# One deferred step for the four state sums of a pair, and a new place for the last two pairs of a retention + bilinear feed-forward kernel

## The chip, the cores and the metric

The kernel runs on one core of one Trainium2 chip. The metric is the device time of one execution in microseconds (us). Four runs of the kernel before gave 336.97, 335.21, 335.25 and 334.94 us: a median of 335.23 us, from 334.94 to 336.97.

TensorE is called PE below, and its weight loads PEld; VectorE is DVE, ScalarE is ACT, GpSimd is POOL, and SyncE, which issues most of the DMAs here, is SP.

## The reference

Two operations in a row. First a retention layer (attention without softmax, with a decay per head) over 8 batches, 8 heads, 576 positions and a head size of 64:

```
scores = (q @ k^T) / 8
ret    = (scores * gamma_h ** (i - j) for i >= j, else 0) @ v       # per batch and head
```

Its output is laid out as 4608 tokens (8 batches x 576) of 512 features and goes into a feed-forward layer without activation:

```
out = ((x @ w_a) * (x @ w_b)) @ w_out        # 512 -> 1536 -> 512
```

All inputs and the output are float32 in DRAM.

## The kernel before

**Tiles.** The tokens are worked on in 18 *pairs* of 256 tokens. A batch has 576 = 2 x 256 + 64 positions, so pairs 0 to 15 are the two halves of each batch (pair n is half n % 2 of batch n // 2), and pairs 16 and 17, from `LEFT` on, gather the last 64 positions of batches 0 to 3 and 4 to 7. `rows_of` (L48) tells for each pair which rows of which batch it holds: two runs of 128 rows for a regular pair, four runs of 64 rows for a left one. A load (`load_pair`, L124) or a store (`store`, L627) issues one DMA per run, tensor and column part.

**Retention by states.** The 256 tokens of a pair are four blocks of 64. Inside a block the kernel uses masked scores; what comes from earlier blocks of the batch enters through a running sum of k^T v, the *state*. For a pair n, `keyed` (L475) makes the four k^T v products of the pair in two PSUM tiles, `kv0` and `kv1` (32 small matmuls, L489). Four instructions of DVE, `add(0)` to `add(3)`, then make the running sums in `sums`: `add(i)` reads the product of block i (`kv0` for i = 0 and 2, `kv1` for i = 1 and 3) and sum i - 1 (L506 for the first block of a batch, L509 for the others). ACT casts the sums to bf16 `states`: sum 1, and sum 3 for the next pair or for the left pairs, in `convert` (L516, L518, L520), and sums 0 and 2, with the partition halves exchanged, in `convert_swapped` (L513). `matched` makes the scores (`sc`, L545), which DVE masks (`sT`, L554); `from_states` (L571) and `from_keys` (L584) make the retention output `o` of a pair, which DVE scales into `xT` (L594). A left pair has nothing to sum: `keyed` returns at once for it, and its states come from `left_states`.

**Feed-forward.** `ffn_block` works on blocks of 512, 256, 256 and then seven times 512 tokens. For each of the 12 slices F of the hidden size: four matmuls into a PSUM tile `pa` (L664), cast by ACT into `ha` (L672); four matmuls into `pb` (L679), multiplied by DVE with `ha` into `hT` (L684). Then, for each 128 tokens, 12 matmuls into `po` (L699), copied by ACT or DVE into `osb` (L708, L710) and stored (L635, L637). The very last 128 tokens are done in two halves of 256 columns, each stored by itself.

**PSUM.** `pa`, `pb`, `po`, `kv0`, `kv1` and the transposes of the start take their space from one pool, `ps_ffn`, of four buffers. A tile takes the buffer whose last reader stands earliest in the recorded order; its first matmul waits for the last reader of the tile that had that buffer. While `kv0` and `kv1` wait for their adds, the feed-forward has the other two buffers.

**Order.** The order of all instructions is written out by hand. PE's queue is that of the feed-forward; `todo` holds the retention work with due times counted in matmuls of 512 columns, and at the edges of the feed-forward what is due is put in. `stretch(into, outof)` (L602) is one such piece: the states part of pair `outof`, then the products and scores of pair `into`, then the keys part of `outof`. From pair 8 on there are two stretches per block: one 116 matmuls before the start of the next block, among its `pa`/`pb` slices, which takes in an odd pair, and one 44 before, among `po`, which takes in an even one. What a stretch leaves for DVE and ACT goes into the list `later` as *deferred steps*, in this order: adds 0 and 1; adds 2 and 3; scaling of `o` (two steps); `convert` with the first mask; `convert_swapped` with the second mask. `pop()` takes one step from the list. In blocks of 512 tokens it is called twice per slice F: after the matmuls of `pa`, before the cast to `ha` is recorded, and after the multiplication into `hT`. In the first three blocks it is called only after `hT`. In `po` it is called after matmuls 3, 6 and 9 and after the copy. The engines run their instructions in the order in which they were recorded; so a step that is popped earlier stands earlier in the queues of DVE and ACT.

Of the kernel before, what the change touches and what calls it, by code (L numbers as in the profile page):

```python
# [18 lines left out]
def kernel(  # L19
# [10 lines left out]
    nc = tc.nc  # L30
# [9 lines left out]
    gammas = [1.0 - 2.0 ** (-5.0 - h) for h in range(H)]  # L40


    NP = NTOK // 256
    LEFT = 2 * B
    FIRST = 3
    assert S == 9 * 64 and B == 8

    def rows_of(n):  # L48

        if n < LEFT:  # L50
            return [(kp, 0, 128, n // 2, 256 * (n % 2) + 128 * kp)
                    for kp in (0, 1)]
        return [(i // 2, 64 * (i % 2), 64, 4 * (n - LEFT) + i, S - 64)
                for i in range(4)]

    def pool(name, bufs, space=None):
# [193 lines left out]

    natural, transposed, scored = {}, {}, {}
    sums_of = {}
    states_of = {LEFT + i: left_states[:, i] for i in (0, 1)}
    later = []

    def pop():
# [77 lines left out]
    def state_step(i, behinds):  # L334

        n, hh = STEPS[i]
        kv = ps_ffn.tile([128, 2, 2, 64], FP32, tag="ab", name="kv0")
        fresh = {0, 1}
        for behind in behinds:
            parts = [(n - 1, slice(0, 128))] if n % 2 else []  # L340
            parts.append((n, slice(0, 128) if behind else half(0)))
            for m, rows in parts:
                qkb, vb = natural[m, hh]
                for j in (0, 1):
                    for kp in (0, 1):
# [12 lines left out]
        if which:  # L358
            w = into[n, which[0]]
            for r in (0, 1):  # L360
                nc.scalar.copy(
                    state_after[half(r), w:w + len(which), cs, half(r)],
                    kv[half(r), which[0]:which[-1] + 1])
        if (n, behinds[-1]) == (1, 1):
            nc.scalar.copy(left_states[:, 0, 0, cs], kv[:, 1])
        elif (n, behinds[-1]) == (FIRST - 1, 1):
            if FIRST not in states_of:
                sums_of[n] = sum_pool.tile([128, 4, HP, 64], FP32,
                                           tag="sums", name="sums")
                states_of[FIRST] = state_pool.tile(  # L370
                    [128, 4, HP, 64], BF16, tag="states", name="states")
            nc.vector.tensor_copy(sums_of[n][:, 3, cs], kv[:, 1])
            nc.scalar.copy(states_of[FIRST][:, 0, cs], kv[:, 1])

    def output_step(i, place=None):
# [41 lines left out]

    def block_of(n, i):

        return 4 * (n % 2) + i if n < LEFT else 8  # L420

    def ahead(n):


        qf, kf, vf = paired.pop(n)
        qkb = nat.tile([128, 2, 2 * DM], BF16, tag="qkb", name="qkb2")
        vb = nat.tile([128, 2 * DM], BF16, tag="vb", name="vb2")
        for w, t in ((0, qf), (1, kf)):
            nc.gpsimd.tensor_copy(qkb[0:64, w], t[0:64])  # L429
            to = qkb[64:128, w].rearrange("p (j r d) -> p j r d", r=2, d=D)  # L430
            fro = t[64:128].rearrange("p (j r d) -> p j r d", r=2, d=D)
            for r in (0, 1):
                nc.gpsimd.tensor_copy(to[:, :, 1 - r], fro[:, :, r])  # L433
        nc.gpsimd.tensor_tensor(  # L434
            vb.rearrange("p (k h d) -> p k h d", k=2, h=H),
            vf.rearrange("p (k h d) -> p k h d", k=2, h=H),
            vs2[:, n % 2 if n < LEFT else 2].unsqueeze(3).to_broadcast([128, 2, H, D]),
            op=ALU.mult)
        natural[FIRST + n, "pair"] = (qkb, vb)

# [25 lines left out]
    def of(store, n):  # L466
        return store[FIRST + n, "pair"]
# [7 lines left out]
    def keyed(n):  # L475


        if n >= LEFT:
            return (lambda: None,) * 2
        qkb, vb = of(natural, n)  # L480
        kvs = [ps_ffn.tile([128, 2, HP, 64], FP32, tag="ab", name=f"kv{a}")
               for a in (0, 1)]
        begun = Begun()
        for kp in (0, 1):
            for c in range(HP):
                for a, r in QUADS:
# [8 lines left out]
        sums_of[n] = sums  # L495
        if n % 2 == 0:
            states_of[n] = state_pool.tile([128, 4, HP, 64], BF16,
                                           tag="states", name="states")
            states_of[n + 1] = state_pool.tile([128, 4, HP, 64], BF16,
                                               tag="states", name="states")  # L500
        into, batch = states_of[n], n // 2

        def add(i):
            own = kvs[i % 2][:, i // 2]
            if block_of(n, i) == 0:
                nc.vector.tensor_copy(sums[:, i], own)  # L506
            else:
                prev = sums[:, i - 1] if i else sums_of[n - 1][:, 3]
                nc.vector.tensor_tensor(sums[:, i], own, prev, op=ALU.add)  # L509

        def swapped(to, fro):
            for r in (0, 1):
                nc.scalar.copy(to(half(1 - r)), fro(half(r)))  # L513

        def convert():
            nc.scalar.copy(into[:, 2], sums[:, 1])  # L516
            if n % 2 == 0:
                nc.scalar.copy(states_of[n + 1][:, 0], sums[:, 3])  # L518
            elif batch % 2 == 0:
                nc.scalar.copy(left_states[:, batch // 4, batch % 4],  # L520
                               sums[:, 3])

        def odd_ones(t, r, i):
            return t[r].rearrange("p (k a) c d -> p a k (c d)", a=2)[:, i]

        def convert_swapped():
            swapped(lambda r: odd_ones(into, r, 1),
                    lambda r: odd_ones(sums, r, 0))
            if n % 2 and batch % 2:
# [47 lines left out]
    def from_keys(n, o, begun):  # L577
        vb = of(natural, n)[1]
        sT = of(scored, n)
        for c in range(HP):  # L580
            for kp in (0, 1):
                for a, r in QUADS:
                    v0 = kp * DM + c * 128 + 64 * r
                    nc.tensor.matmul(o[half(r), a, c, kp, :],  # L584
                                     vb[half(a), v0:v0 + 64],
                                     sT[half(a), r ^ a, c, kp, :],
                                     start=begun.first(a, r), stop=True,
                                     skip_group_check=True)
        s0 = 64 * block_of(n, 0)
        step = 128 if n < LEFT else 0  # L590
# [297 lines left out]
```

## Time and profile before

| | before |
|---|---|
| median of four runs | 335.23 us |
| the profiled execution, its own time | 336.97 us |
| its span in the trace | 335.3 us |
| PE busy | 327.2 us (98%) |
| DVE busy | 162.8 us (49%) |
| ACT busy | 128.0 us (38%) |
| POOL busy | 114.9 us (34%) |
| adds of states, L506 and L509 | 6 x 424 ns and 46 x 424 ns (medians) |
| multiplication into hT, L684 | 120, mean 633 ns |
| cast to ha, L672 | 120, mean 542 ns |

The profiled execution is the one of 336.97 us, the slowest of the four; 1.7 us of it lie around the span. A matmul of the trace has the time from its start to the end of its result, and the next one starts before that end; so PE counts as busy where it in fact waits a little. How fast PE goes is read from the starts: four 512-column matmuls of a `pa` or `pb` take 0.86 us from the first start to the start of what follows, four of 256 columns 0.43 us.

### The profile page before, as it was taken

The page shows a single profiled execution, that of the slowest core. Times are in us where ns is not written, and L with a number is a line of the kernel's source. Part 1 is how long each engine was busy: PE and PEld are TensorE (multiplying, and loading weights), DVE is VectorE, ACT ScalarE, POOL GpSimd, SP SyncE. Part 2 cuts the span into 40 slices and gives each one's busy share as a digit, 9 for nine tenths or more (in the row PEclk, how much of TensorE's full clock was granted, in tenths as well). Part 3 has the DMA queues.
Part 4 walks back from the last instruction along what each step waited for, and adds up shares of the span by engine and source line. Part 5 has one row for each costly group of instructions (what it writes and reads, how often), then busy time and mean ns, then how long its engine had stood idle before and what let it go on. Part 6 is the DMA issues. An engine that isn't in the chain of part 4 may idle for free.

```text
span 335.3 us, 8707 instructions
## 1 busy us (share of the span) xinstructions
PE 327.2 (98%) x3648; PEld 168.5 (50%) x3648; DVE 162.8 (49%) x292; ACT 128.0 (38%) x275; POOL 114.9 (34%) x146
## 2 busy tenths in 40 slices
PE   7999999999999999999999999999999999999994
PEld 4644446857644554545454545454544444444443
DVE  5724445466746465566246624762475145314420
ACT  7634743444525244353235323532262123213311
POOL 4770068550547468445054505450420000000000
PEclk9979999999999999999999999999999999999999
DMA  7999999997999999993599259955850510020014
GB/s 210 252 162 207 253 232 220 217 170 118 202 198 226 225 215 254 229 214 81 132 228 208 54 136 234 168 78 148 178 115 2 143 47 0 2 104 23 1 31 94
DMA packets 143191, 50.37 MB, mean 150 GB/s; under 512 B 124592, under 2 KB 138672, under 8 KB 143152
## 3 DMA queue, kind: packets, MB, share of 16 engines
q1 hardware_dynamic: 138400, 45.10, 65.9%
q0 software_dynamic: 4752, 4.72, 8.6%
q8 instruction: 28, 0.46, 0.6%
q14 instruction: 11, 0.09, 0.1%
HBM read 37.75 MB, written 9.44 MB: 141 GB/s over the span
## 4 chain that ended last, share of the span: by engine, by line
PE 92%; SPq 2%; DMA 2%; ACT 1%; DVE 0%; issue 0%; ACTq 0%; DVEq 0%
PE po L699 28%; PE pb L679 28%; PE pa L664 28%; SPq L142 2%; DMA vf<-in_v_dram 2%; PE o L584 2%; PE o L571 1%; PE sc L545 1%; PE kv L489 1%; PE pa L646 1%; PE kv L348 1%; PE o L398 1%; PE o L389 0%; ACT vb L296 0%; ACT osb L708 0%
## 5 line engine op out<-in xcount | busy, mean ns | idle before, releaser
L684 DVE TENSOR_TENSOR hT<-ha,pb 128x512 bf16<-128x512 bf16 (+1 forms) x120 | 75.8, 633 | 99.2 <-PE pb L679 90.1
L672 ACT CAST ha<-pa 128x512 bf16<-128x512 f32 (+1 forms) x120 | 64.7, 542 | 125.6 <-PE pa L664 124.9
L679 PE MATMUL pb<-xT,wb_sb 128*128 128x512 bf16 (+1 forms) x480 | 111.8, 358 | 0.1
L664 PE MATMUL pa<-xT,wa_sb 128*128 128x512 bf16 (+1 forms) x474 | 110.3, 358 | 0.2
L699 PE MATMUL po<-wo_sb,hT 128*128 128x512 bf16 (+1 forms) x444 | 97.5, 374 | 0.0
L679 PEld LDWEIGHTS <-wb_sb 128*128 128x128 bf16 x480 | 46.7, 98 | 47.6 <-issue 1.6
L664 PEld LDWEIGHTS <-wa_sb 128*128 128x128 bf16 x474 | 45.3, 98 | 46.0 <-issue 1.3
L699 PEld LDWEIGHTS <-hT 128*128 128x128 bf16 x444 | 42.2, 98 | 46.9
L429 POOL CAST qkb<-qf 64x1024 bf16<-64x1024 f32 x15 | 15.5, 1031 | 91.3 <-DMA qf<-in_q_dram 75.5
L710 DVE COPY osb<-po 128x512 f32<-128x512 f32 (+1 forms) x18 | 12.2, 676 | 42.0 <-PE po L699 42.0
L434 POOL TENSOR_TENSOR vb<-vf,vs 128x1024 bf16<-128x1024 f32 x15 | 28.5, 1902 | 9.6 <-PE o L584 5.3
L708 ACT COPY osb<-po 128x512 f32<-128x512 f32 (+1 forms) x19 | 10.9, 574 | 47.5 <-PE po L699 47.5
L594 DVE TENSOR_TENSOR xT<-o,qs 128x512 bf16<-128x512 f32 x30 | 19.6, 682 | 7.1 <-PE o L584 7.1
L509 DVE TENSOR_TENSOR sums<-kv,sums 128x256 f32<-128x256 f32 x46 | 19.4, 422 | 1.7
L554 DVE TENSOR_TENSOR sT<-sc,mask 128x512 bf16<-128x512 f32 x30 | 19.7, 680 | 0.0
L433 POOL CAST qkb<-kf 64x512 bf16<-64x512 f32 x30 | 17.7, 616 | 0.8
L433 POOL CAST qkb<-qf 64x512 bf16<-64x512 f32 x30 | 17.6, 616 | 0.6
L429 POOL CAST qkb<-kf 64x1024 bf16<-64x1024 f32 x15 | 15.5, 1036 | 3.6 <-DMA kf<-in_k_dram 3.0
L513 ACT CAST states<-sums 64x512 bf16<-64x512 f32 x26 | 16.0, 617 | 0.4
L288 POOL CAST qkb<-kf 128x512 bf16<-128x512 f32 x5 | 3.1, 616 | 18.9 <-DMA kf<-in_k_dram 18.9
L723 PE MATMUL w<-ones 128*128 128x256 bf16 (+1 forms) x36 | 7.8, 342 | 1.5 <-DVE ones L186 1.5
L328 DVE TENSOR_TENSOR sT<-sc,mask_s 128x1024 bf16<-128x1024 f32 x6 | 7.3, 1220 | 1.7 <-PE sc L320 1.7
(81 smaller groups left out, 158.3 us busy)
## 6 DMA issues: line engine op xcount, KB each, us to landing
qf<-in_q_dram SPq DMA_DIRECT2D x32, 256.0 KB, 4.4
kf<-in_k_dram SPq DMA_DIRECT2D x32, 256.0 KB, 5.0
vf<-in_v_dram SPq DMA_DIRECT2D x32, 256.0 KB, 5.1
out_dram<-osb SPq DMA_DIRECT2D x26, 256.0 KB, 2.2
out_dram<-osb SPq DMA_DIRECT2D x18, 128.0 KB, 2.4
wo_sb<-in_moe_w_out_dram POOLq DMA_DIRECT2D x3, 512.0 KB, 16.6
qf<-in_q_dram SPq DMA_DIRECT2D x8, 128.0 KB, 3.4
kf<-in_k_dram SPq DMA_DIRECT2D x8, 128.0 KB, 3.7
```

Source lines behind the costliest of these rows:

```text
L429: nc.gpsimd.tensor_copy(qkb[0:64, w], t[0:64])
L433: nc.gpsimd.tensor_copy(to[:, :, 1 - r], fro[:, :, r])
L434: nc.gpsimd.tensor_tensor(vb.rearrange("p (k h d) -> p k h d", k=2, h=H), vf.rearrange("p (k h d) -> p k h d", k=2, h=H), vs2[:, n % 2 if ...
L509: nc.vector.tensor_tensor(sums[:, i], own, prev, op=ALU.add)
L513: nc.scalar.copy(to(half(1 - r)), fro(half(r)))
L554: nc.vector.tensor_tensor(sT[:, on].rearrange("p c k s -> p (c k) s"), sc[:, on].rearrange("p c k s -> p (c k) s"), mask3.unsqueeze(1).to_ ...
L594: nc.vector.tensor_tensor(x_of(t0, 128).rearrange("p c (a s) -> p c a s", a=2), o[:, :, :, kp].rearrange("p a c s -> p c a s"), qs[:, :, s ...
L664: nc.tensor.matmul(pa[:, 0:n], wa_sb[:, c, fs], xT[:, c], start=(c == 0), stop=(c == NC - 1))
L672: nc.scalar.copy(ha[:, 0:n], pa[:, 0:n])
L679: nc.tensor.matmul(pb[:, 0:n], wb_sb[:, c, fs], xT[:, c], start=(c == 0), stop=(c == NC - 1))
L684: nc.vector.tensor_tensor(hT[:, F, 0:n], has[F][:, 0:n], pb[:, 0:n], op=ALU.mult)
L699: nc.tensor.matmul(po[:, 0:width], hT[:, F, u * 128:(u + 1) * 128], wo_sb[:, F, cols], start=(F == 0), stop=(F == NF - 1))
```

## The change

1. *Adds.* `later` gets one step with all four adds, where it had two steps with two each. Every later step of that stretch moves one pop earlier.
2. *Order of the pairs.* `LEFT` becomes `{15: 0, 17: 1}`: pair 15 is now the left pair of batches 0 to 3, and pair 16 the second half of batch 7 (`regular(16)` is 15). Pair 17 stays the left pair of batches 4 to 7. So pair 14 is followed, within its batch, by pair 16 (`then`), and the products of batch 7's second half are made in the stretch that takes in pair 16 and no longer in the one that takes in pair 15.
3. *Places in x.* `place` exchanges the places of pairs 16 and 17 in `xT` and in the stores: tokens 4096 to 4351 of the order in x are pair 17, the last 256 are pair 16. The last 128 tokens are then rows of one batch, and each of the two column halves of the end is one store of 128 rows in place of two of 64 rows.

The dictionary `sums_of` has other keys; nothing else is computed differently.

```diff
-    LEFT = 2 * B
+    LEFT = {NP - 3: 0, NP - 1: 1}
+    def regular(n):
+        return n - (n > NP - 3)
+
+    def place(n):
+        return n if n < NP - 2 else 2 * NP - 3 - n
+
     def rows_of(n):
-        if n < LEFT:
-            return [(kp, 0, 128, n // 2, 256 * (n % 2) + 128 * kp)
+        if n not in LEFT:
+            m = regular(n)
+            return [(kp, 0, 128, m // 2, 256 * (m % 2) + 128 * kp)
                     for kp in (0, 1)]
-        return [(i // 2, 64 * (i % 2), 64, 4 * (n - LEFT) + i, S - 64)
+        return [(i // 2, 64 * (i % 2), 64, 4 * LEFT[n] + i, S - 64)
                 for i in range(4)]
...
     def keyed(n):
-        if n >= LEFT:
+        if n in LEFT:
             return (lambda: None,) * 2
+        m, batch = regular(n) % 2, regular(n) // 2
+        then = n + 1 + (n + 1 in LEFT)
...
-        if n % 2 == 0:
+        if m == 0:
             states_of[n] = state_pool.tile([128, 4, HP, 64], BF16,
                                            tag="states", name="states")
-            states_of[n + 1] = state_pool.tile([128, 4, HP, 64], BF16,
-                                               tag="states", name="states")
+            states_of[then] = state_pool.tile([128, 4, HP, 64], BF16,
+                                              tag="states", name="states")
...
-        later.append(lambda: (add(0), add(1)))
-        later.append(lambda: (add(2), add(3)))
+        later.append(lambda: [add(i) for i in range(4)])
         return convert, convert_swapped
...
         def scaled(kp):
-            t0 = n * 256 + kp * 128
+            t0 = place(n) * 256 + kp * 128
...
     def store(u, cols, osb):
-        n, u = u // 2, u % 2
+        n, u = place(u // 2), u % 2
```

More of the change, by code (lines that the diff above doesn't have):

```diff
@@ L252 @@
     sums_of = {}
-    states_of = {LEFT + i: left_states[:, i] for i in (0, 1)}
+    states_of = {n: left_states[:, i] for n, i in LEFT.items()}
     later = []
@@ L367, in state_step @@
             if FIRST not in states_of:
-                sums_of[n] = sum_pool.tile([128, 4, HP, 64], FP32,
+                sums_of[1, 0] = sum_pool.tile([128, 4, HP, 64], FP32,
                                            tag="sums", name="sums")
@@ L371, in state_step @@
                     [128, 4, HP, 64], BF16, tag="states", name="states")
-            nc.vector.tensor_copy(sums_of[n][:, 3, cs], kv[:, 1])
+            nc.vector.tensor_copy(sums_of[1, 0][:, 3, cs], kv[:, 1])
             nc.scalar.copy(states_of[FIRST][:, 0, cs], kv[:, 1])
@@ L418, in block_of @@
     def block_of(n, i):
-        return 4 * (n % 2) + i if n < LEFT else 8
+        return 8 if n in LEFT else 4 * (regular(n) % 2) + i
     def ahead(n):
@@ L436, in ahead @@
             vf.rearrange("p (k h d) -> p k h d", k=2, h=H),
-            vs2[:, n % 2 if n < LEFT else 2].unsqueeze(3).to_broadcast([128, 2, H, D]),
+            vs2[:, 2 if n in LEFT else regular(n) % 2].unsqueeze(3).to_broadcast([128, 2, H, D]),
             op=ALU.mult)
@@ L494, in keyed @@
         sums = sum_pool.tile([128, 4, HP, 64], FP32, tag="sums", name="sums")
-        sums_of[n] = sums
-        if n % 2 == 0:
+        before, sums_of[batch, m] = sums_of.get((batch, 0)), sums
+        if m == 0:
             states_of[n] = state_pool.tile([128, 4, HP, 64], BF16,
                                            tag="states", name="states")
-            states_of[n + 1] = state_pool.tile([128, 4, HP, 64], BF16,
-                                               tag="states", name="states")
-        into, batch = states_of[n], n // 2
+            states_of[then] = state_pool.tile([128, 4, HP, 64], BF16,
+                                              tag="states", name="states")
+        into = states_of[n]
         def add(i):
@@ L507, in add @@
             else:
-                prev = sums[:, i - 1] if i else sums_of[n - 1][:, 3]
+                prev = sums[:, i - 1] if i else before[:, 3]
                 nc.vector.tensor_tensor(sums[:, i], own, prev, op=ALU.add)
@@ L516, in convert @@
             nc.scalar.copy(into[:, 2], sums[:, 1])
-            if n % 2 == 0:
-                nc.scalar.copy(states_of[n + 1][:, 0], sums[:, 3])
+            if m == 0:
+                nc.scalar.copy(states_of[then][:, 0], sums[:, 3])
             elif batch % 2 == 0:
@@ L528, in convert_swapped @@
                     lambda r: odd_ones(sums, r, 0))
-            if n % 2 and batch % 2:
+            if m and batch % 2:
                 swapped(lambda r: left_states[r, batch // 4, batch % 4],
                         lambda r: sums[r, 3])
-        later.append(lambda: (add(0), add(1)))
-        later.append(lambda: (add(2), add(3)))
+        later.append(lambda: [add(i) for i in range(4)])
         return convert, convert_swapped
@@ L589, in from_keys @@
         s0 = 64 * block_of(n, 0)
-        step = 128 if n < LEFT else 0
+        step = 0 if n in LEFT else 128
         def scaled(kp):
-            t0 = n * 256 + kp * 128
+            t0 = place(n) * 256 + kp * 128
             nc.vector.tensor_tensor(
```

## The prediction, made before the changed kernel was run

> **What bounds the kernel now.** I read the page first (span, busy shares, granted clock), then the chain of waits over the whole span, then the chain and the timeline of the stretches it shows as uneven, and last the timeline and the DMA table at the end.
>
> ```profile
> span 335.3 us, 8707 instructions
> PE 327.2 (98%) x3648; PEld 168.5 (50%) x3648; DVE 162.8 (49%) x292; ACT 128.0 (38%) x275; POOL 114.9 (34%) x146
> PEclk9979999999999999999999999999999999999999
> ```
>
> PE is the bound all the way at a granted clock of nine tenths or more from about 25 us on; all others have half their time free. The change gives PE the same 3648 matmuls, so it can only gain or lose where PE waits a fraction of a microsecond inside its "busy" time, and behind the last matmul. The chain of waits (start, length, instruction) shows where that is in the 512-token blocks:
>
> ```profile
> 101.14 0.86 PE pb L679 x4
> 102.00 0.86 PE pa L664 x4
> 102.87 1.01 PE pb L679 x4
> ...
> 243.44 1.01 PE pb L679 x4
> ```
>
> Four 512-column matmuls take 0.86; the pb at 102.87 takes 1.01. The same 1.01 stands at 141.57, 175.49, 209.41 and 243.44: five times 0.15, each in the third slice after a stretch that took in a pair. The timeline there (start, length, engine, line) says why:
>
> ```profile
> 100.74 0.43 DVE L509 TENSOR_TENSOR sums<-kv,sums 128x256 f32<-128x256 f32 x1
> 102.11 0.69 DVE L684 TENSOR_TENSOR hT<-ha,pb 128x512 bf16<-128x512 bf16 x1 [0.95 <-PE pb L679]
> 102.72 0.88 DVE L509 TENSOR_TENSOR sums<-kv,sums 128x256 f32<-128x256 f32 x2
> 102.85 1.02 PE L679 MATMUL pb<-xT,wb_sb 128*128 128x512 bf16 x4
> ```
>
> Adds 2 and 3 come after the next hT, so kv0 and kv1 still hold two of the four buffers, and pb takes the one that hT is reading until 102.80; it starts 0.05 later. DVE had been idle 0.95 before that hT.
>
> In the 256-token blocks the chain leaves PE:
>
> ```profile
> 67.01 0.42 DVE hT L684
> 67.43 0.34 DVE sums L509
> 67.78 0.02 issue
> 67.80 0.34 DVE sums L509
> 68.15 0.04 issue
> 68.19 0.43 DVE hT L684
> 68.62 0.04 issue
> 68.67 0.60 PE pb L679 x4
> ```
>
> Here a pb waits for an hT that stands behind two adds. At the end:
>
> ```profile
> 331.05 0.37 ACT L708 COPY osb<-po 128x256 f32<-128x256 f32 x1 [2.04 <-PE po L699]
> 331.53 1.18 SPq L637 DMA_DIRECT2D out_dram<-osb  x2
> ...
> out_dram<-osb SPq DMA_DIRECT2D x26, 256.0 KB, 2.2
> out_dram<-osb SPq DMA_DIRECT2D x18, 128.0 KB, 2.4
> out_dram<-osb SPq DMA_DIRECT2D x4, 64.0 KB, 2.0
> ```
>
> The last copy ends at 331.42; SP then issues two stores, the second at 332.13, and 2.04 later it has landed (334.17). The rest to 335.3 is the closing of the program.
>
> **The change, part by part.**
>
> *1a. Adds in one go, 512-token blocks.* The step is popped after the pa of the first slice, ahead of its hT. At 100.22 DVE starts add 0; four dependent ones at a pitch of 0.45 end near 102.0, before that hT can start (102.11, it waits for pb): they fill the 0.95 of idle time. At the other four places the first two adds end earlier against hT (at 241.17 with hT at 242.68), so the cover is wider, 1.51 against 0.9 needed. Both kv buffers are free before the second pa, and by the built program's bank numbers pb of that slice takes one of them and waits for nothing recent. Gain: 4 x 0.15 = 0.60. Each later step moves up by one pop (convert and its ACT copies, scaling, masks); DVE and ACT have a hole of about 1 us in every slice here, and no PE instruction then waits longer. In po, where four stretches take in an even pair (124, 154, 188 and 222 us), and after the one at 115.9, the chain shows no wait (one unbroken piece of 9.60 for 44 matmuls of po), a po tile lives 2.6, and I take nothing.
>
> *1b. Adds in one go, 256-token blocks.* These are three stretches (kv at 65.2, 78.3 and 85.2), with pops only after hT and 0.43 per pa or pb. PE waits at the second and third slice after them: pa for ACT's cast, pb for hT. At 65 to 69 us those waits add up to 0.19, 0.13, 0.06 and 0.25, from starts of 66.93, 67.49, 67.98 and 68.67 against 0.43 each. The first three stand before the adds or beside them and stay. The fourth pb now takes kv0's buffer and waits for add 2, not for hT. Before, that wait was add, add, hT (the chain above: 67.43 to 68.62). After, it is add, add, add: 67.35 + 0.45 + 0.45 + 0.42 = 68.67, and 0.05 to PE. That is 68.72 against 68.67: +0.05 to +0.08, say +0.07, and three times: +0.2. Then DVE is behind by hT and add 3, but the reader of those hT slices, po, needs them only at its 11th and 12th matmul, 2.2 us on.
>
> The second stretch (78.3) has more slices behind it, not po. Deferred steps come one slice earlier while the adds end no earlier, so ACT's queue changes: the two swapped casts (0.62 each) now stand ahead of the cast of the fourth slice. From the rows there: add 3 ends at 82.3, the state copy behind it at 82.7, ha (0.37) at 83.0, the swapped casts (1.25 for two, 0.1 of each overlapped) at 84.1, ha of slice four at 84.4. The pa two slices on has that buffer and would start at 84.17; it starts at 84.45: +0.28. Sum of 1b: +0.5. Bounds: +0.2 if that pa finds its buffer free, +1.0 if hT, late by two adds, holds up a further pb at each (0.2 to 0.3 a time).
>
> *A rule against it.* In the chain above hT at 68.19 starts only when both adds before it are done. The Trainium skill, page "PSUM — Partial Sum Buffer", section "Engine vs sequencer instructions", says that the queues of ScalarE and VectorE are strictly first in, first out; by that alone two more adds ahead of hT, 0.85, would be paid at each of the three stretches, +2.5 in place of +0.2. The rows decide by what PE waits for: add 2 of kv0's buffer, not the late hT.
>
> *2. Pairs 15 and 16 change roles.* The stretch at 239.3 loses its 32 kv matmuls, its adds and so the fifth wait of 0.15; they move to the one at 255.6, in po, where the same work at 153.7, 187.6 and 221.6 shows no wait. PE's total is the same. The wait of from_keys for ACT's fence copy where nothing stands between, about 0.13, moves with it (two such stretches before, two after). Pair 15's loads are now the 12 DMAs of 64 rows (9.1 us of SP issue at 233.7), pair 16's the 6 of 128; they, the transposes behind them and the two casts of states move by one pair, some 34 us of cover against about 3 us in the scores that wait for the transposes at 239.8. Four stores of block seven become eight, behind all loads. Taken: -0.15; bounds -0.15 and +0.3 (a late transpose).
>
> *3. The last store.* One store of 128 rows is issued at 331.53 instead of two. The issue at 332.13 goes: 0.60 earlier. Its landing is not in the trace for 128 x 256; the nearest rows are 64 x 256 (2.0 us), 64 x 512 (2.4, the same bytes) and 128 x 512 (2.2, the same rows and twice the bytes). I take 2.2: landing at 333.73 against 334.17, -0.44. One more closing wait of SP stands behind the last landing, about 0.05. Taken: -0.4; bounds -0.6 and -0.15.
>
> The Trainium skill, page "DMA: Bandwidth & Descriptors", section on the anatomy of one DMA, fits a DMA of the GpSimd path as 2.0 us plus the bytes over 436 GB/s; for 128 KB against 64 KB that would be an estimated 0.15 more, and the saving about 0.4. No run here shows that shape.
>
> **Sum.** -0.60 + 0.5 - 0.15 - 0.4 = -0.65 us, -0.2%. The profiled execution took 336.97 us (span 335.3 and 1.7 around it), the slowest of the four; its forecast is 336.3. Against the median of 335.23, which is 0.5% below it, the same 0.65 gives 334.6.
>
> **The rivals.**
>
> *A, dearer adds (slower).* One mechanism: at 66 to 90 us a pb needs the buffer that the late hT still reads, so that all four adds lie in PE's way. It decides from the point where the wait per stretch exceeds 0.6 (1.75 in all, that is 1.35 of gains plus 0.4, to be no gain); at two adds, 0.85 x 3 + 0.28 = 2.8, it gives 2.8 - 0.6 - 0.15 - 0.4 = +1.65: 336.9. For it: DVE runs without a hole there (67.01 to 68.62). Against: the bank of that pb in the built program. Two more adds are the most it can be.
>
> *B, all gain.* The later waits of 1b do not come, as ACT and DVE catch up, and the last store lands after 2.0: -0.6 + 0 - 0.15 - 0.6 = -1.35: 333.9. For it: PE's waits on ACT are of 0.1 to 0.3, the size of my errors. Against: ACT's queue order.
>
> *C, it does nothing.* The 0.15 waits turn into others of the same size (a cast to ha behind an early convert), and 3 is the only gain: +0.5 - 0.4 = +0.1: 335.3. For it: ACT's waits at 102 to 104 already show casts displaced by state copies. Against: two free buffers more.
>
> **How the numbers follow.** Mine 0.6, B 0.17, C 0.15, A 0.08. About 0.5% (1.7 us) is what a measurement of this kernel can tell from no change. The terms' own bounds add to -1.3 and +0.5 without A, so 333.9 to 335.7; with the spread of three of the runs (334.94 to 335.25) the range is 333.5 to 335.7. A's end stays outside. Faster than 333.55 takes B with more: 0.1. Slower than 336.9 takes A at its full price or more: 0.05. The rest is 0.85.
>
> **What would show it.** In the chain, 0.86 where 1.01 stood at five places; the sums as one row of four adds (about 1.8) ahead of hT; around 84.4 a pa late by 0.3; po starting within 0.1 of 69.1; kv at 255 and none at 239; one store of 128 x 256 as the last issue, landing 2.0 to 2.4 after it, and the span's end 0.4 nearer to the last ACT copy. Wrong if a row at 66 to 90 us shows pb behind four adds and an hT, or a new wait for a DMA shows on PE after 200 us.

## The result, and the profile after

The changed kernel takes 334.20 us (median of 43 runs) against 335.17 us for the kernel before (median of 64 runs beside it). The ratio is 0.9973 with a 95% interval of 0.9963 to 0.9983: 0.9 us, or 0.3%, less. The forecast was 334.6 us, between 333.5 and 335.7, and "within 0.5%" with a chance of 0.85. The total was met to 0.4 us. Two of its four terms were not: one loss was larger than forecast and one gain much larger, and the two errors partly cancel, so that the total came out this close is in part luck. One run of all, in the third measurement of the changed kernel, took 476.94 us at a granted clock of 0.659; that row's median would be 334.02 us without it, and its ratio leaves it out.

The page of the changed kernel has the same work on every engine, as forecast:

```profile
span 332.7 us, 8708 instructions
PE 325.4 (98%) x3648; PEld 168.0 (50%) x3648; DVE 163.8 (49%) x292; ACT 128.2 (39%) x275; POOL 114.9 (35%) x146
PEclk9999999999999999999999999999999999999999
```

Its profiled execution took 334.39 us, 1.7 us more than its span. The spans of the two profiles differ by 2.6 us (335.3 and 332.7), and most of that is not the change. The page of before reads 9979 where this one reads 9999: in the slice with the 7, TensorE was granted less clock, and the first key products of a deferred pair (line 489 before, 500 after) start at 65.19 us there and at 63.45 us here, behind work that the change does not touch. In the profiles of the experiments that follow, whose pages all read 9999, they start at 62.7 to 63.6 us, with either form of the adds. So I compare from these key products on, in three parts (the copy between the last two, 0.37 us in both, is left out):

| us | before | after | difference | forecast |
|---|---|---|---|---|
| three 256-token stretches (65.19 to 99.43 before, 63.45 to 98.45 after) | 34.25 | 35.00 | +0.75 | +0.5 |
| from there to the start of the last output copy of ACT | 231.62 | 230.96 | -0.66 | -0.75 |
| end of that copy to the end of the span | 3.83 | 2.89 | -0.94 | -0.4 |
| sum | | | -0.85 | -0.65 |

**512-token blocks.** The chain of waits of the changed kernel (start, length, instruction) where the fourth of the five short waits stood:

```profile
205.41 0.97 PE pa L674 x4
206.38 0.86 PE pb L689 x4
207.25 0.86 PE pa L674 x4
208.11 0.86 PE pb L689 x4
```

In the chain of before the last two of these pieces read as follows:

```profile
208.54 0.86 PE pa L664 x4
209.41 1.01 PE pb L679 x4
```

The 1.01 is 0.86 now, and so it is at all five places (the stretch at the fifth has no adds any more); counted from start to start, these pb stood about 0.147 us late before. The DVE timeline at the first of the places (start, length, engine, line) shows the cover that this needed:

```profile
99.75 1.34 DVE L520 TENSOR_TENSOR sums<-kv,sums 128x256 f32<-128x256 f32 x3
101.13 0.69 DVE L694 TENSOR_TENSOR hT<-ha,pb 128x512 bf16<-128x512 bf16 x1
```

The adds end at 101.09 and hT starts 0.04 us later, with no wait named: the idle 0.95 us that stood ahead of this hT before is used up to the last.

**256-token blocks.** The chain at the first stretch:

```profile
65.28 0.42 DVE hT L694
65.70 0.34 DVE sums L520
66.04 0.02 issue
66.06 0.43 DVE sums L520
66.50 0.02 issue
66.52 0.43 DVE sums L520
66.96 0.05 issue
67.00 0.61 PE pb L689 x4
67.61 2.60 PE po L709 x12
```

It is hT, add, add, add, pb, as forecast (before: hT, add, add, hT, pb), and po follows without a wait. At the second stretch stands the late pa. The timeline, with the idle time of an engine and what ended it in brackets:

```profile
80.67 0.40 ACT L529 CAST states<-sums 128x256 bf16<-128x256 f32 x1 [0.57 <-DVE sums L520]
80.99 0.36 ACT L682 CAST ha<-pa 128x256 bf16<-128x256 f32 x1
81.38 1.25 ACT L524 CAST states<-sums 64x512 bf16<-64x512 f32 x2
82.53 0.63 ACT L682 CAST ha<-pa 128x256 bf16<-128x256 f32 x2
82.94 0.60 PE L674 MATMUL pa<-xT,wa_sb 128*128 128x256 bf16 x4 [0.38 <-ACT ha L682]
```

ACT runs the two swapped casts (81.38 to 82.63), and only then the cast to ha whose end frees the buffer of this pa. Counted from start to start the pa is 0.54 us late; the view's 0.38 leaves out the pipelining of the matmuls. In the kernel before, the same casts stand one slice later:

```profile
83.33 1.25 ACT L513 CAST states<-sums 64x512 bf16<-64x512 f32 x2
83.99 0.60 PE L664 MATMUL pa<-xT,wa_sb 128*128 128x256 bf16 x4
84.48 0.63 ACT L672 CAST ha<-pa 128x256 bf16<-128x256 f32 x2
```

The pa at 83.99 is the last one ahead of the next stretch, so no pa waits for the casts to ha that stand behind them there.

**The end.** The timeline of the last copy and the last store:

```profile
329.41 0.37 ACT L718 COPY osb<-po 128x256 f32<-128x256 f32 x1 [2.04 <-PE po L709]
329.81 0.33 SPq L647 DMA_DIRECT2D out_dram<-osb  x1
```

The row of its size in the DMA table (KB each, median us to landing):

```profile
out_dram<-osb SPq DMA_DIRECT2D x22, 128.0 KB, 2.4
```

One store stands where before had two at 331.53. It takes 0.33 us to issue, where the 64-row stores of before took 0.55 to 0.59, and lands 1.71 us after its start, where the last of before took 2.04. The median of 2.4 in the table is that of the 64x512 stores, which are 20 of the 22, and says nothing about it.

### The profile page after: what moved, and what is told of

Same layout as the page of the kernel before. It is cut to its first block, busy times and chain, and to the rows that moved or that the text cites. A ratio compares the mean times of both kernels' runs of the same rounds, so it can differ in the third digit from the quotient of the medians.

```text
span 332.7 us, 8708 instructions
## 1 busy us (share of the span) xinstructions
PE 325.4 (98%) x3648; PEld 168.0 (50%) x3648; DVE 163.8 (49%) x292; ACT 128.2 (39%) x275; POOL 114.9 (35%) x146
## 4 chain that ended last, share of the span: by engine, by line
PE 91%; SPq 2%; DMA 2%; DVE 2%; ACT 1%; issue 1%; ACTq 0%; DVEq 0%
PE po L709 28%; PE pb L689 27%; PE pa L674 27%; SPq L151 2%; DMA vf<-in_v_dram 2%; PE o L594 2%; PE o L581 2%; PE sc L555 1%; PE kv L500 1%; DVE sums L520 1%; PE kv L357 1%; PE pa L656 0%; DVE hT L694 0%; PE o L407 0%; ACT vb L305 0%
## 5 line engine op out<-in xcount | busy, mean ns | idle before, releaser
L733 PE MATMUL w<-ones 128*128 128x256 bf16 (+1 forms) x36 | 8.6, 370 | 1.5 <-DVE ones L195 1.5
L623 ACT COPY fence<-o 128x2 f32<-128x2 f32 x15 | 2.4, 161 | 15.3 <-PE o L581 15.3
```

## The experiments

My theory: the adds in one go gain 0.15 us at each 512-token place and lose about as much in the 256-token stretches, by the late pa above all; the exchange of the pairs is worth 0.15 us; the rest, the larger half, is the last store. The rivals: that the adds carry the gain; that the early waits cost nothing in the end; that the store gains by having fewer DMAs in flight, or by its bytes, rather than by its shape.

The table has the readings of all profiles, in the same parts (the second one split, for a reason that the row of split early adds brings up). "Early" is the three 256-token stretches. "115-136" is the time from the small products at about 115 us to those at about 136 us (114.76 and 136.45 in the changed kernel). "Rest" is all other time from the end of the early stretches to the start of the last output copy of ACT, and "end" what follows that copy. The time is the median of each kernel's runs, the ratio that to the kernel before on the same chip.

| kernel | early | 115-136 | rest | end | time, us | ratio to before [95%] |
|---|---|---|---|---|---|---|
| before | 34.25 | 21.69 | 209.94 | 3.83 | 335.17 | |
| after | 35.00 | 21.69 | 209.27 | 2.89 | 334.20 | 0.9973 [0.9963, 0.9983] |
| adds only | 35.00 | 21.69 | 209.22 | 3.83 | 335.24 | 1.0012 [0.9995, 1.0030] |
| order only | 34.24 | 21.74 | 209.83 | 2.89 | 334.24 | 0.9972 [0.9959, 0.9984] |
| no exchange in x | 34.99 | 21.82 | 209.26 | 3.83 | 335.16 | 1.0001 [0.9989, 1.0014] |
| store only | 34.24 | 22.02 | 209.94 | 2.97 | 333.94 | 0.9965 [0.9944, 0.9986] |
| one half store | 34.25 | 22.13 | 209.96 | 3.18 | 334.54 | 0.9981 [0.9971, 0.9992] |
| last store in two | 35.04 | 21.74 | 209.27 | 3.11 | 334.50 | 0.9981 [0.9967, 0.9996] |
| split early adds | 34.25 | 22.41 | 209.26 | 2.88 | 333.58 | 0.9961 [0.9947, 0.9976] |
| split early adds, again | 34.25 | 22.26 | 209.26 | 2.90 | 333.66 | 0.9954 [0.9938, 0.9971] |
| empty step | 34.53 | 21.69 | 209.26 | 2.87 | 333.46 | 0.9947 [0.9932, 0.9962] |
| adds at once | 33.51 | 21.74 | 209.24 | 2.90 | 332.70 | 0.9923 [0.9910, 0.9936] |
| after, again | 35.00 | 21.93 | 209.26 | 2.88 | 334.28 | 0.9967 [0.9955, 0.9979] |
| after, once more | 35.00 | 22.11 | 209.24 | 2.88 | 334.10 | 0.9966 [0.9950, 0.9982] |

The columns are worth a look by themselves. "Early" and "rest" repeat to some hundredths of a microsecond from profile to profile and follow the program alone, so terms of 0.1 us can be read there that no comparison of times could show.

### The adds alone

```diff
--- before
-        later.append(lambda: (add(0), add(1)))
-        later.append(lambda: (add(2), add(3)))
+        later.append(lambda: [add(i) for i in range(4)])
```

> The kernel before with the first edit alone: all four adds in one deferred step, pairs and places as before. My reading of the changed kernel's trace is that the five waits of 0.15 us in the 512-token blocks go (-0.73) and that the three stretches among the 256-token blocks pay it back (+0.07, +0.58 and +0.02, in all +0.67). So -0.06 us: the same time as before, ratio 0.9998, with the pb at the five places back at 0.86 and a pa about 0.5 late in the second early stretch. Rival: the adds are what made the changed kernel faster, and this one alone gives at least half of its gain, 0.5 us or more, ratio 0.9985 or less.

Measured: 335.24 us, ratio 1.0012. The five waits are gone and "rest" falls by 0.72 us, "early" grows by 0.75 and the end stays at 3.83. The chain at the first of the five places:

```profile
99.80 0.86 PE pb L678 x4
100.66 0.86 PE pa L663 x4
101.52 0.86 PE pb L678 x4
```

So the edit that names the change is worth nothing in time: it takes away five waits of 0.15 us and puts as much into one late pa and three later pb.

### The order alone

```diff
--- after
-        later.append(lambda: [add(i) for i in range(4)])
+        later.append(lambda: (add(0), add(1)))
+        later.append(lambda: (add(2), add(3)))
```

> The changed kernel with the adds as before, in two deferred steps: the new roles of pairs 15 and 16 and the new places alone. If the end is what pays: the part behind the last ACT copy is 2.9 us long as in the changed kernel, against 3.8 before (-0.93), and the one wait of 0.15 at the stretch that took in pair 15 goes (-0.15): -1.1 us, ratio 0.9968, slightly below the changed kernel. Rival, the forecast's sizes: the last store saves 0.4 and this kernel 0.55, ratio 0.9984, and is slower than the changed kernel.

Measured: 334.24 us, ratio 0.9972, the whole gain. Four of the five waits remain, as in this piece of its chain, and the fifth is gone; "early" is that of before, the end that of after.

```profile
99.52 0.86 PE pa L675 x4
100.38 1.01 PE pb L690 x4
```

### The new order without the exchange of places in x

```diff
--- after
     def place(n):
-        return n if n < NP - 2 else 2 * NP - 3 - n
+        return n
```

> The changed kernel without the exchange of places: pair 16 is still the second half of batch 7 but lies before pair 17 in x, so the last 128 tokens are again four-run rows of a left pair and each half of the end is stored with two DMAs of 64 rows. If the last store is nearly all of the gain, this one has the time of before: -0.73 + 0.67 and nothing else, ratio 0.9998, 3.8 us behind the last ACT copy. Rival, the roles of the pairs matter by themselves: the gain of the changed kernel stays in half or more, ratio 0.9986 or less.

Measured: 335.16 us, ratio 1.0001: everything else of the change is there, and it gains nothing. The rows stored last are 64-row pieces again, and the end is 3.83.

### The store alone

```diff
--- before
         n, u = u // 2, u % 2
+        if n == NP - 1 and u == 1:
+            nc.sync.dma_start(out[NTOK - 128:NTOK, cols], osb[:, cols])
+            return
```

> The kernel before with one edit at its end: each half of the last 128 tokens goes out with one DMA of 128 rows, to 128 rows that follow each other in out and are not those that these tokens belong to, so the last rows of the output are wrong. All other instructions are as before. If one store of 128 rows in place of two of 64 is what pays at the end, -0.9 us (0.6 of the second issue, 0.34 of a landing of 1.7 in place of 2.0, 0.08 as SP is no longer late for the last part, less 0.07 in the closing), ratio 0.9972. Rival, forecast's size: -0.4, ratio 0.9988, with a landing of 2.0 or more.

Measured: 333.94 us, ratio 0.9965. Nothing but the shape of the last stores differs from before, and the end falls from 3.83 to 2.97 us. The last copy and store in its timeline:

```profile
329.79 0.37 ACT L711 COPY osb<-po 128x256 f32<-128x256 f32 x1 [2.03 <-PE po L702]
330.19 0.34 SPq L630 DMA_DIRECT2D out_dram<-osb  x1
```

It lands 1.73 us after its start, against 2.04 for the 64-row store of before. So the store is sufficient for the gain, and with the experiment before it also necessary. One row does not fit the shape alone. The store of the first half has the same 128 rows of 256 columns, but starts 0.10 us behind the end of the issue of a 64-row store:

```profile
328.99 0.53 SPq L630 DMA_DIRECT2D out_dram<-osb  x1
```

It takes 0.53 us to issue and 2.10 to land, as much as a 64-row one. What stands right ahead of a store counts too, and why is not shown.

### One of the two 64-row stores left out

```diff
--- before
+            if n == NP - 1 and u == 1 and r0 == 64:
+                continue
```

> The kernel before without the second of the two 64-row stores in each half of the last 128 tokens, so 64 rows of the output are never written. It splits the end's gain into the issue that goes and the form of the store that stays. If the number of rows matters, the store that stays still takes 0.55 to issue and lands 2.0 after its start: 0.60 + 0.08 gained, -0.65 us, ratio 0.998, 3.15 us behind the last ACT copy. Rival, it is only that fewer stores are in flight: it lands in 1.7 too and the gain is that of the one store of 128 rows, -0.9 us, ratio 0.997.

Measured: 334.54 us, ratio 0.9981, end 3.18: 0.65 us of the end go with the second store. The one 64-row store that remains has nothing behind it:

```profile
329.68 0.47 SPq L639 DMA_DIRECT2D out_dram<-osb  x1
```

It takes 0.47 us to issue and 1.95 us to land, not much less than as one of two (0.55 and 2.02, 0.59 and 2.04). The fair match for it is the last store of "store only": the same place and the same columns, and SP had issued nothing for 0.66 and 0.67 us before each. With 128 rows that one took 0.34 to issue and 1.73 to land, at twice the bytes. That two were in flight together explains at most 0.1 us of the 0.34 us by which the 128-row store lands sooner.

### The last store in two, of 128 rows each

```diff
--- after
-                nc.sync.dma_start(rows, osb[r0:r0 + m, cols])
+                for c0 in (range(cols.start, cols.stop, 128) if cols.start
+                           else (cols.start,)):
+                    c1 = c0 + 128 if cols.start else cols.stop
+                    nc.sync.dma_start(out[b * S + s0:b * S + s0 + m, c0:c1],
+                                      osb[r0:r0 + m, c0:c1])
```

> The changed kernel with its very last store (128 rows of 256 columns, 128 KB) cut into two of 128 rows and 128 columns (64 KB each, as many bytes as each of the two 64-row stores that closed the kernel before). It tells what makes the 64-row stores dear. If it is their rows (half the partitions), each of the two issues in 0.34 us and the last lands in 1.7 us, so the end behind the last output copy of ACT grows from 2.89 to about 3.25 us: ratio 0.9980. If it is the bytes or the number of stores, they behave as the 64-row ones did (0.55 to 0.59 us to issue, 2.0 us to land) and the end is 3.75 to 3.83 us: ratio 0.9996.

Measured: 334.50 us, ratio 0.9981, end 3.11. The timeline:

```profile
328.94 0.37 ACT L722 COPY osb<-po 128x256 f32<-128x256 f32 x1 [2.04 <-PE po L713]
329.33 0.81 SPq L650 DMA_DIRECT2D out_dram<-osb  x2
...
out_dram<-osb SPq DMA_DIRECT2D x2, 64.0 KB, 1.6
```

The two take 0.33 and 0.42 us to issue and 1.54 and 1.61 us to land. They have exactly the bytes of the two 64-row stores of before and are as many, yet the last lands at 2.02 us behind the end of the copy, where the last of before landed at 2.74 us. So neither the bytes nor the number of stores makes the 64-row ones dear: it is what a store of half the partitions takes. These rows are also half as long (512 bytes against 1 KB), and part of the 0.72 us is that: behind the end of their issue the two land in 1.19 and 1.21 us, where the last store of the changed kernel takes 1.38. What the rows cost is mostly in the issue. Of the 0.34 us by which the last store of the changed kernel lands sooner after its start than that of before, 0.25 is the shorter issue (0.33 against 0.59 us) and 0.08 comes behind it (1.38 against 1.45). Why half the rows take longer to issue, no view shows.

### The early adds in two steps, the later ones in one go

```diff
--- after
-        later.append(lambda: [add(i) for i in range(4)])
+        if n < FIRST + 3:
+            later.append(lambda: (add(0), add(1)))
+            later.append(lambda: (add(2), add(3)))
+        else:
+            later.append(lambda: [add(i) for i in range(4)])
```

> The changed kernel with the adds in two deferred steps as before for pairs 3, 4 and 5 (the stretches among the 256-token blocks), and in one step for all others. If the early stretches pay back what the 512-token blocks gain, this is 0.67 us faster than the changed kernel: ratio to before 0.995, about 333.5 us. Rival: the late pa and pb of the early stretches are covered by something later, and the time is that of the changed kernel, 0.997.

Measured: 333.58 us, ratio 0.9961. "Early" is back at 34.25, 0.75 us less, and the five waits stay away. The median is 0.70 us below that of the changed kernel on the same chip; but the intervals of the two ratios overlap, and the total of its profile did not show the gain, since "115-136" had grown from 21.69 to 22.41. So it was measured again, and the changed kernel with it:

> The changed kernel with the adds of the three 256-token stretches in two steps as before the change and in one go elsewhere, measured a second time with more rounds beside the changed kernel itself. By the waits in the traces (0.627, 0.680 and 0.679 us early against 0.70, 1.256 and 0.703) it is 0.67 us faster than the changed kernel: ratio to the kernel before 0.9949 against 0.9969. Its first profile did not show this gain in the total because of a stall of 0.63 us among the small products at 122 to 124 us for which the profile names no cause; in a profile without that stall the time from the first key products to the last output copy of ACT is 265.3 us. Rival: the early waits cost nothing in the end, ratio 0.9969.

> The changed kernel itself, beside the three others, so that these are compared on one chip: ratio 0.9969, end behind the last output copy of ACT 2.89 us, late pa 0.54 us. If the stall at 122 to 124 us is chance, it is anywhere from nothing to 0.6 us in this profile; if it belongs to the program, it is the same as in the earlier profiles of the changed kernel (0 and 0.25 us already differ).

Measured: 333.66 us and 0.9954 for the split, 334.10 us and 0.9966 for the changed kernel. The two intervals overlap again, so the times alone do not show the gain; "early" does. The stall is there again in the split (22.26), and the waits of PE name it only as time in which the engine waited for nothing that the profile shows:

```profile
PE o L598 <- issue: 0.4, 1, 0.4
```

It does not belong to the split alone: the kernels "store only" and "one half store", which do at that time exactly what before does, show 22.02 and 22.13 where before shows 21.69, and three profiles of the changed kernel show 21.69, 21.93 and 22.11. So it varies from one execution to the next by up to 0.4 us with one and the same program. Both profiles of the split have more than any other (0.57 and 0.72 us over the least), so a part of it may belong to that program; what it is stays open. Without the stall the profile agrees with the waits: from the first key products to the last copy 265.77 - 0.57 = 265.20 us, against 265.96.

The changed kernel was also run beside the split the first time:

> The changed kernel once more, beside the next three on one chip, as their yardstick: ratio 0.997 to before, 2.9 us behind the last ACT copy, the pa about 0.5 us late in the second early stretch.

Measured: 334.28 us, ratio 0.9967, with the same late pa (0.539 us) and an end of 2.88.

### An empty step behind the adds of the second stretch

```diff
--- after
         later.append(lambda: [add(i) for i in range(4)])
+        if n == FIRST + 1:
+            later.append(lambda: None)
```

> The changed kernel with an empty deferred step put behind the adds of the pair of the second 256-token stretch, so that the adds stay in one go while every later step of that stretch (masks, casts, scalings) has the slice that it had before the change. If the late pa of that stretch (0.54 us at 82.94 in the trace of the changed kernel) comes from the two swapped casts moving up one slice, as the forecast has it, that wait is gone, the 0.27 us of the fourth pb stays, and the stretch from its key products to the next small stretch falls from 7.27 us to 6.73 us: ratio to the kernel before 0.9952 against 0.9969 for the changed kernel, 333.6 us. Rival: the adds in one go make pa late by themselves (DVE's 1.77 us of adds push its later work back); then the 0.54 us stays with the spacer, 7.27 us and 0.9969.

Measured: 333.46 us, ratio 0.9947; this interval too overlaps that of the changed kernel beside it. But the stretch falls from 7.27 to 6.72 us, and the chain runs through the place without ACT; all that is left in this piece is the wait of the fourth pb (the one at 79.77):

```profile
79.77 0.61 PE pb L691 x4
80.38 0.44 PE pa L676 x4
80.81 0.44 PE pb L691 x4
81.25 0.44 PE pa L676 x4
81.69 0.44 PE pb L691 x4
82.12 0.44 PE pa L676 x4
82.56 0.44 PE pb L691 x4
83.00 0.30 PE o L583 x20
```

The adds are still in one go, so it is not they that make pa late. It is what stands behind them, which a shorter list of steps moved up one slice. The empty step holds back both `convert` and the swapped casts; that it is the swapped casts, the timeline of the changed kernel shows (81.38 to 82.63, right ahead of the cast to ha that the pa waits for). Where they stood before, PE went on with the small products of `o`, which take their buffer from another pool.

### The adds at once

```diff
--- after
-        later.append(lambda: [add(i) for i in range(4)])
+        for i in range(4):
+            add(i)
```

> The changed kernel with no deferred step for the adds at all: they are recorded in keyed itself, right behind the matmuls of kv0 and kv1, for every pair. In the early stretches DVE then starts them about 1.2 us earlier, while PE is still at the scores, and both kv buffers are free before the second slice, so most waits there go (0.70 at the first, 1.26 at the second, 0.70 at the third, less about 0.8 that stays as the next hT is late): -1.9 us against the changed kernel, ratio to before 0.9915, about 332.3 us. Rival: the adds, now ahead of the hT of the running slice, hold that hT up and with it pb or po, and the time is that of the changed kernel or more, 0.997 and up.

Measured: 332.70 us, ratio 0.9923, faster than both kernels. "Early" falls to 33.51 us, 1.49 below after and 0.74 below before; "rest" is unchanged. The chain at the first stretch:

```profile
64.94 0.44 DVE sums L520
65.38 0.05 issue
65.43 0.61 PE pa L675 x4
66.04 0.44 PE pb L690 x4
66.47 0.44 PE pa L675 x4
66.91 0.44 PE pb L690 x4
```

PE waits once, 0.43 us, for an add, and none of the next slices waits; it waited four times there in before (0.63 in all) and four times in after (0.70). The four adds are now queued ahead of the hT of the first slice instead of behind it. The buffers of the key products come free that much sooner, and hT, though late, holds up nobody there. The gain was expected larger (-1.9 us): in the three stretches together 1.15 us of waits remain, not 0.8, as the second begins with a wait of 0.43 us too.

## Why the prediction was right, point by point

**1a, the five waits: right.** Forecast -0.60 for four of them, measured 0.147 us each; the fifth was counted under 2. The adds end 0.04 us ahead of hT at the place with the least cover, as the working had it (102.0 against 102.11).

**1b, the 256-token stretches: right in mechanism and sign, too small.** Forecast +0.5, measured +0.75. The start-to-start waits of PE in the slices concerned add up to 0.63, 0.68 and 0.68 us before and to 0.70, 1.26 and 0.70 after: +0.67. The rest of the 0.75 is hundredths at other slices. The fourth pb was put at +0.07 each; the stretches with their other slices, but without the late pa, grew by 0.07, 0.04 and 0.02. The undersized term is the late pa: +0.28 forecast, 0.54 measured. Its place, its cause and its chain of steps were as the working had them. In the time of the kernel before (the key products of this stretch start at 78.28 us there and 76.63 here, so 1.65 us on), the steps agree with it up to the ha ahead of the swapped casts: add 3 ended at 82.24 (forecast 82.3), the second state copy at 82.73 (82.7), ha at 83.00 (83.0). The later ones came late: the swapped casts ended at 84.27 (84.1), the next ha at 84.54 (84.4), and pa started at 84.59 (84.45). These 0.14 us are the swapped casts: two of them take 1.25 us from first start to last end, and behind the ha they begin only when it has ended; I had let them overlap with it. The other 0.12 us lie in the start that this pa would have without the wait: forecast 84.17, but the slices ahead of it were slower by 0.06 us only, not by 0.18, so it was 84.05. The stated bound of +1.0 held.

**The rule against it** (the Trainium skill, "PSUM — Partial Sum Buffer", section "Engine vs sequencer instructions", on queues that are strictly first in, first out) would have made 1b +2.5, at 0.85 us of adds per stretch in PE's way. What the runs show: hT did start only behind the adds queued ahead of it, and what that cost depended on which buffer the waiting matmul takes. With the adds at once, all four stand ahead of an hT and the stretches become 0.74 us shorter than before; where PE waits in the chain shown there, it waits for an add of the key products and not for hT. The queue order alone does not price it.

**2, the exchange of the pairs: right.** Forecast -0.15. "Order only" against before: "rest" falls by 0.11, with the fifth wait of 0.147 gone and some hundredths added. No transpose came late, so the bound of +0.3 was not needed.

**3, the last store: the step that failed, by its size.** Forecast -0.4 with bounds of -0.6 and -0.15, measured -0.94, outside the bounds. Its terms:

| us | forecast | measured |
|---|---|---|
| second issue gone | -0.60 | -0.60 |
| landing of the last store, against 2.04 | +0.16 (taken as 2.2) | -0.34 (1.71) |
| SP free when the copy ends | not counted | -0.08 |
| one more closing wait | +0.05 | +0.07 |

(The sum of the forecast was rounded to -0.4.) The landing was priced by the nearest rows, and all three misled. The 64x256 row has half the rows, and a half-height store turns out slow; the 64x512 row has the same fault, with rows twice as long; the 128x512 row has long rows too, and its median (2.2) is over stores of which several ran beside loads (up to 5.5 us), while those from 290 us on landed in 2.00 to 2.04, in the trace of before already. None of them was a lower bound, so the 2.0 behind the bound of -0.6 was not the least that this store could take. The 0.08 stood in the trace of before: the store at 331.53 began 0.10 us after the copy's end, where it begins 0.03 after it now, because SP was still issuing the second half of the store before it, until 331.44. "DMA: Bandwidth & Descriptors" of the Trainium skill, section on the anatomy of one DMA, gives for the GpSimd path a fit by which 128 KB would be an estimated 0.15 us slower than 64 KB; no run here has a store on that path. From SP, a store of 128 rows landed 0.34 us sooner than one of 64 rows at twice the bytes, so the bytes alone do not order these, and the measurement decides. Among stores of 128 rows the bytes do count, and by about as much as the estimate: 64 KB landed in 1.54 and 1.61 us, 128 KB in 1.71.

**The rivals.** A (a pb behind the late hT, +1.65) did not come: the fourth pb waits for an add, as the chain shows. C (the waits come back, only the store gains) is nearest: over the whole program the adds gain nothing, and the end's 0.94 us is more than the total of 0.85. Its mechanism was not the one at work: the waits that come back are not casts in the 512-token blocks, where the gain stays, but the wait for one cast in a 256-token stretch, and smaller ones of the fourth pb. B's total (333.9) lies as near to the result as mine, but the later waits that it left out did come.

**The range.** The lower bounds of the terms add to -0.60 + 0.2 - 0.15 - 0.6 = -1.15 us, not to the -1.3 of the working; the measured time lies inside either way. Rival A's threshold of 0.6 us per stretch does not follow from its own gains either (0.6 + 0.15 + 0.4 = 1.15 us over three stretches is 0.38); no such wait came.

So the total was met because an error of +0.25 in 1b and one of -0.54 in 3 partly cancel, with 0.09 from the five waits and the exchange: -0.65 + 0.25 - 0.54 + 0.09 = -0.85 us. That cancelling is luck; the mechanisms of 1a, 1b and 2 are not.

## What to carry to other kernels

In a list of deferred steps, shortening the list moves every later step. Price a change of it by what each of the steps behind will stand next to, not by the step that is edited; here an empty step was worth 0.55 us of profile, and the better form was not to defer the adds at all. At the very end of a program, read the last transfer by itself: its issue and its landing are paid in full, and the shape of the store sets both (0.94 us here), while the gain of five waits of 0.15 us inside the bound engine went, for the most part, into one wait (0.54 us) behind two casts that had moved. And where a term is to be read in tenths of a microsecond, compare intervals between fixed anchors of two traces, which repeated here to some hundredths outside one piece (115 to 136 us), and not their spans.

## What the runs showed of the hardware that was not expected

- A store of 64 partitions is dearer than one of 128, at half the bytes. From SP at the end of the program: 64x256 float32 (64 KB) takes 0.47 to 0.59 us to issue and 1.95 to 2.07 to land; 128x256 (128 KB) 0.33 to 0.34 and 1.70 to 1.76, with one exception (0.53 and 2.10, right behind a 64-row store); 128x128 (64 KB) 0.33 and 0.42, 1.54 and 1.61. The issue shows the same for stores of 512 columns: from 290 us on in the changed kernel, those of 128 rows issue in 0.33 to 0.34 us and those of 64 rows in 0.47 to 0.60.
- Most of that is the issue. From its end to the landing, rows of 1 KB take 1.45 to 1.48 us with 64 rows and 1.36 to 1.43 with 128 (the exception 1.57); rows of 2 KB take 1.76 to 1.80 and 1.66 to 1.71.
- PE stalled between 115 and 136 us by 0 to 0.4 us in executions of programs that are identical there, and by up to 0.7 us in one other kernel, with no releaser in the profile.
- The start of the program, up to the first key products at about 63 us, varied by 2.5 us between profiles (62.7 to 65.2), with the granted clock lower in the longest one. That is more than all terms of this change together.
